# Decode attention on one Trainium2 core: one head per transfer, keys on partitions, whole-row softmax

## The chip, the cores and the metric

One core of a Trainium2 chip runs the whole program. The metric is device time in microseconds (us) of one execution. A core has TensorE (PE, with its weight loads shown apart as PEld), VectorE (DVE), ScalarE (ACT), GpSimd (POOL) and SyncE (SP), and 16 DMA engines that fill its on-chip memory.

## The reference

A layer norm of `x`, then attention with a K/V cache (one query per batch) and a SwiGLU network side by side, both added to `x`. Batch 4, width 512, 32 heads, 8192 keys of 128 numbers, all bf16:

```python
def _A_ref(x, k_cache, v_cache, wq, wo):          # B, Sq, D = 4, 1, 512;  H, Sk, Dh = 32, 8192, 128
    q = (lambda x, *d: x.transpose(*d))((x @ wq).reshape(B, Sq, H, Dh), 0, 2, 1, 3)
    scores = jnp.einsum("bhqd,bhkd->bhqk", q, k_cache) * (Dh ** -0.5)
    p = _softmax(scores, axis=-1)
    o = jnp.einsum("bhqk,bhkd->bhqd", p, v_cache)
    return (lambda x, *d: x.transpose(*d))(o, 0, 2, 1, 3).reshape(B, Sq, H * Dh) @ wo
def _B_ref(x, w_gate, w_up, w_down):              # F = 1792
    g = _silu(x @ w_gate)
    u = x @ w_up
    return (g * u) @ w_down
...
xn = _layernorm(x, axis=-1)
return x + _A_ref(xn, A_k_cache, A_v_cache, A_wq, A_wo) + _B_ref(xn, B_w_gate, B_w_up, B_w_down)
```

There are 4 x 32 = 128 pairs of a batch and a head, called heads here. Each has 2 MiB of K and 2 MiB of V, so 512 MiB of cache pass through the core once.

## The kernel before

It goes over the 8192 keys in four chunks `j` of 2048 (`CH`), and over all 128 heads within each chunk.

- `k_phase(j)` loads K for two heads (`HG`) of one batch with one 1 MiB transfer on SP's queue (tile `knat`, in runs of 4 KB). K comes with keys on partitions. TensorE turns each block of 128 keys by a transpose, K block stationary and an identity moving (line 231), into PSUM tiles `tps` of eight blocks. `evac` copies them to `kt`, three of five on DVE (line 113), two on ACT (line 115). Then the scores: q of the head, alone in a 32-column block `qpad`, is stationary, and 512 columns of `kt` move. Four batches use four column strips of the array, and the results add up in four PSUM tiles `sps`, with heads on partitions. All heads' scores of a chunk go to `s_buf`, with their running maximum.
- `softmax_phase(j)` is an online softmax for all 128 heads at once: new maximum, a factor `ccol` that rescales the output so far (`OT`) and the row sums (`RST`), exp on ACT (line 270), and transposes of the result (line 275), so that `pt_buf` has keys on partitions.
- `pv_phase(j)` loads V as K is loaded (tile `vt`) and multiplies: a 128x128 block of V is stationary, one column of `pt_buf` moves, and the result adds to a column of `OT` in PSUM tile `mp`.

All matmuls but the transposes go through one helper, `mm_acc` (line 118), and so have its line. After the first `k_phase`, the `pv_phase` of chunk j and the `k_phase` of chunk j+1 alternate, two heads of each batch at a time (a group `g`); the last `pv_phase` has no K beside it. There, `wo` is loaded on ACT's queue, and `finalize_group` normalizes and multiplies by it. The weights of the network are loaded at the start on ACT's queue and used before the first chunk. The order within each engine is that of the program; K and V tiles wait on SP for one of 5 (`knat`) or 8 (`vt`) buffers.

Of the kernel before, what the change touches and what calls it, by code (L numbers as in the profile page):

```python
# [8 lines left out]
dt = mybir.dt  # L10
# [6 lines left out]
def kernel(  # L17
# [20 lines left out]
    assert D % P == 0 and F % P == 0  # L38
# [3 lines left out]
    T = 16  # L42
    CH = P * T
    assert Sk % CH == 0
    NJ = Sk // CH
    HG = 2
    assert H % HG == 0
    NG = H // HG
    SB = 512
    NA = CH // SB  # L50
    assert NA * SB == CH and 32 * B == P
    EB = 1024
    assert CH % EB == 0 and EB % P == 0
    NEB = CH // EB
    TPB = EB // P
    assert T % TPB == 0
    NTC = CH // P
    eps = 1e-5
    qscale = float(Dh) ** -0.5
    NKN = 5  # L60
    NKT = 6
    NV = 8
    assert FC % 7 == 0
# [6 lines left out]
    v_pool = ctx.enter_context(tc.tile_pool(name="vnat", bufs=NV))  # L70
    psM = ctx.enter_context(tc.tile_pool(name="psM", bufs=1, space=bass.MemoryType.PSUM))
# [5 lines left out]
    ones_pb = const.tile([P, 1], dt.bfloat16, name="ones_pb")  # L77
    nc.vector.memset(ones_pb[:], 1.0)
    ones_row = const.tile([1, P], dt.float32, name="ones_row")
    nc.vector.memset(ones_row[:], 1.0)  # L80

    qpad = persist.tile([P, M * 32], dt.bfloat16, name="qpad")
    s_buf = [persist.tile([P, CH], dt.bfloat16, name=f"s_buf{i}") for i in range(2)]
    pt_buf = [persist.tile([P, NTC, P], dt.bfloat16, name=f"pt_buf{i}") for i in range(2)]
    xnt = persist.tile([P, EC, B], dt.bfloat16, name="xnt")
    yfx = persist.tile([B, D], dt.float32, name="yfx")
    cmaxj = persist.tile([P, 1], dt.float32, name="cmaxj")
    cmax4 = persist.tile([P, NA], dt.float32, name="cmax4")
    mrun = persist.tile([P, 1], dt.float32, name="mrun")
    mnew = persist.tile([P, 1], dt.float32, name="mnew")  # L90
    ccol = persist.tile([P, 1], dt.float32, name="ccol")
    nbias = persist.tile([P, 1], dt.float32, name="nbias")
    row_sb = persist.tile([1, P], dt.float32, name="row_sb")
    bc_sb = persist.tile([P, M], dt.float32, name="bc_sb")
    otn_sb = persist.tile([P, M], dt.bfloat16, name="otn_sb")

    mp = psM.tile([P, 512], dt.float32, name="mp")
    OT = mp[:, 0:M]
    BC = mp[:, 128:128 + M]
    RST = mp[0:1, 256:256 + M]  # L100
    CT = mp[0:1, 384:384 + M]
    nc.vector.memset(mp[:, 0:256], 0.0)
    nc.vector.memset(mp[0:1, 256:512], 0.0)

    nc.gpsimd.memset(qpad[:], 0.0)

    copy_i = [0]

    def evac(out_ap, in_ap):
        k = copy_i[0] % 5  # L110
        copy_i[0] += 1
        if k in (0, 2, 4):
            nc.vector.tensor_copy(out=out_ap, in_=in_ap)  # L113
        else:
            nc.scalar.copy(out=out_ap, in_=in_ap)  # L115

    def mm_acc(out_ap, lhsT, rhs, **kw):
        nc.tensor.matmul(out_ap, lhsT=lhsT, rhs=rhs, start=False, stop=False,  # L118
                         skip_group_check=True, **kw)

    def col_stride_ap(ap2d, start, count, step):
        return ap2d[:, start : start + step * (count - 1) + 1 : step]

    def bcast_row(row_src_ap):
        nc.vector.memset(BC, 0.0)
        mm_acc(BC, lhsT=ones_row[0:1, :], rhs=row_src_ap)
        nc.vector.tensor_copy(out=bc_sb[:], in_=BC)

    with tc.tile_pool(name="knat", bufs=NKN) as knat_pool, \
            tc.tile_pool(name="kt", bufs=NKT) as kt_pool, \  # L130
            tc.tile_pool(name="psT", bufs=3, space=bass.MemoryType.PSUM) as psT:
        with tc.tile_pool(name="p0sb", bufs=1) as p0, tc.tile_pool(name="p0ps", bufs=1, space=bass.MemoryType.PSUM) as p0ps:
            x_sb = p0.tile([B, D], dt.bfloat16, name="x_sb")
            nc.sync.dma_start(out=x_sb[:], in_=x_flat[:, :])
            wq_c, wg_c, wu_c = [], [], []
            for c in range(EC):
                t_ = kt_pool.tile([P, H * Dh], dt.bfloat16, name="kt")
                nc.sync.dma_start(out=t_[:], in_=A_wq[c * P:(c + 1) * P, :])
                wq_c.append(t_)
            for c in range(EC):  # L140
                t_ = knat_pool.tile([P, F], dt.bfloat16, name="knat")
                nc.scalar.dma_start(out=t_[:], in_=B_w_gate[c * P:(c + 1) * P, :])
                wg_c.append(t_)
            for c in range(EC):
                t_ = v_pool.tile([P, F], dt.bfloat16, name="vt")
                nc.scalar.dma_start(out=t_[:], in_=B_w_up[c * P:(c + 1) * P, :])
                wu_c.append(t_)
            wd_c = []
            for fc2 in range(0, FC, 7):
                t_ = v_pool.tile([P, 7, D], dt.bfloat16, name="vt")  # L150
                nc.scalar.dma_start(out=t_[:], in_=B_w_down[fc2 * P:(fc2 + 7) * P, :].rearrange(
                    "(fc p) e -> p fc e", p=P))
                wd_c.append(t_)

            xf = p0.tile([B, D], dt.float32, name="xf")
            nc.vector.tensor_copy(out=xf[:], in_=x_sb[:])
            xsum = p0.tile([B, 1], dt.float32, name="xsum")
            nc.vector.reduce_sum(out=xsum[:], in_=xf[:], axis=AX.X)
            mean = p0.tile([B, 1], dt.float32, name="mean")
            nc.vector.tensor_scalar(out=mean[:], in0=xsum[:], scalar1=1.0 / D, scalar2=None, op0=ALU.mult)  # L160
            xc = p0.tile([B, D], dt.float32, name="xc")
            nc.vector.tensor_scalar(out=xc[:], in0=xf[:], scalar1=mean[:, 0:1], scalar2=None, op0=ALU.subtract)
            sq = p0.tile([B, D], dt.float32, name="sq")
            nc.vector.tensor_tensor(out=sq[:], in0=xc[:], in1=xc[:], op=ALU.mult)
            vsum = p0.tile([B, 1], dt.float32, name="vsum")
            nc.vector.reduce_sum(out=vsum[:], in_=sq[:], axis=AX.X)
            epst = p0.tile([B, 1], dt.float32, name="epst")
            nc.vector.memset(epst[:], eps)
            std = p0.tile([B, 1], dt.float32, name="std")
            nc.scalar.activation(out=std[:], in_=vsum[:], func=ACT.Sqrt, bias=epst[:, 0:1], scale=1.0 / D)  # L170
            rstd = p0.tile([B, 1], dt.float32, name="rstd")
            nc.vector.reciprocal(out=rstd[:], in_=std[:])
            xn_bf = p0.tile([B, D], dt.bfloat16, name="xn_bf")
            nc.vector.tensor_scalar(out=xn_bf[:], in0=xc[:], scalar1=rstd[:, 0:1], scalar2=None, op0=ALU.mult)

            xnt_ps = p0ps.tile([P, EC, B], dt.bfloat16, name="xnt_ps")
            for c in range(EC):
                nc.tensor.transpose(xnt_ps[:, c, :], xn_bf[0:B, c * P:(c + 1) * P], ident[0:B, 0:B])
            nc.vector.tensor_copy(out=xnt[:], in_=xnt_ps[:])

            qt_ps = p0ps.tile([P, H * B], dt.float32, name="qt_ps")
            nc.vector.memset(qt_ps[:], 0.0)
            for h in range(H):
                for c in range(EC):
                    mm_acc(qt_ps[:, h * B:(h + 1) * B], lhsT=wq_c[c][:, h * Dh:(h + 1) * Dh], rhs=xnt[:, c, :])
            for b in range(B):
                dst = col_stride_ap(qpad[:], b * H * 32, H, 33)
                src = col_stride_ap(qt_ps[:], b, H, B)
                nc.vector.tensor_scalar(out=dst, in0=src, scalar1=qscale, scalar2=None, op0=ALU.mult)

            gu_ps = p0ps.tile([P, 2, FC * B], dt.float32, name="gu_ps")
            nc.vector.memset(gu_ps[:], 0.0)
            for fc in range(FC):
                for c in range(EC):
                    mm_acc(gu_ps[:, 0, fc * B:(fc + 1) * B], lhsT=wg_c[c][:, fc * P:(fc + 1) * P], rhs=xnt[:, c, :])
            for fc in range(FC):
                for c in range(EC):
                    mm_acc(gu_ps[:, 1, fc * B:(fc + 1) * B], lhsT=wu_c[c][:, fc * P:(fc + 1) * P], rhs=xnt[:, c, :])
# [8 lines left out]
            for fc in range(FC):  # L207
                mm_acc(yf_ps[0:B, :], lhsT=ht[:, fc * B:(fc + 1) * B], rhs=wd_c[fc // 7][:, fc % 7, :])
# [88 lines left out]
        def run_all(gen):  # L297
            for _ in gen:
                pass
# [66 lines left out]
```

## Time and profile before

| | |
|---|---|
| Runs | 1423.69 us median of 3 (1423.33 to 1423.88) |
| Profiled execution | span 1421.1 us from its first to its last instruction; its time outside the span is not in the profile, and the runs' median is 2.6 us longer |
| TensorE matmuls, busy | 1181.8 us (83%) |
| TensorE weight loads, busy | 896.6 us (63%) |
| DVE, ACT busy | 464.5 us (33%), 428.4 us (30%) |
| Moved by DMA | 553.37 MB, mean 389 GB/s |
| Mean granted TensorE clock | 0.829 |

In a profile row, `x` and a number is a count; "busy" is the union of the instructions' times, and "mean" that of one, in ns. A matmul's row names its stationary block as partitions*columns, then its output and its type. "PEclk" is the share of its full clock that TensorE was granted. A matmul's own duration includes its latency; in a burst, matmuls overlap, so the time each adds is less than its duration. After `[` stands the idle time ahead, and what ended it.

### The profile page before, as it was taken

The page shows a single profiled execution, that of the slowest core. Times are in us where ns is not written, and L with a number is a line of the kernel's source. Part 1 is how long each engine was busy: PE and PEld are TensorE (multiplying, and loading weights), DVE is VectorE, ACT ScalarE, POOL GpSimd, SP SyncE. Part 2 cuts the span into 40 slices and gives each one's busy share as a digit, 9 for nine tenths or more (in the row PEclk, how much of TensorE's full clock was granted, in tenths as well). Part 3 has the DMA queues.
Part 4 walks back from the last instruction along what each step waited for, and adds up shares of the span by engine and source line. Part 5 has one row for each costly group of instructions (what it writes and reads, how often), then busy time and mean ns, then how long its engine had stood idle before and what let it go on. Part 6 is the DMA issues. An engine that isn't in the chain of part 4 may idle for free.

```text
span 1421.1 us, 40337 instructions
## 1 busy us (share of the span) xinstructions
PE 1181.8 (83%) x18861; PEld 896.6 (63%) x18861; DVE 464.5 (33%) x790; ACT 428.4 (30%) x435; POOL 4.5 (0%) x9
## 2 busy tenths in 40 slices
PE   2999999899988988898898898799888889854454
PEld 2666666677766666676666666677666666643333
DVE  2444444433323332532233233433233323320000
ACT  0444445333323332432233233333223323310000
POOL 1000000000000000000000000000000000000000
PEclk9999999898888888898888788889888878855555
DMA  9988889899999999999999999999999999999997
GB/s 379 364 322 316 318 324 353 355 408 408 408 409 408 408 408 408 403 409 408 408 408 408 402 408 402 408 380 408 408 408 408 408 406 408 381 373 408 409 408 297
DMA packets 147158, 553.37 MB, mean 389 GB/s; under 512 B 8488, under 2 KB 14384, under 8 KB 146480
## 3 DMA queue, kind: packets, MB, share of 16 engines
q1 hardware_dynamic: 139856, 541.11, 96.3%
q10 hardware_dynamic: 7136, 9.70, 2.0%
q8 instruction: 147, 2.41, 0.7%
q14 instruction: 19, 0.16, 0.0%
HBM read 550.77 MB, written 0.00 MB: 388 GB/s over the span
## 4 chain that ended last, share of the span: by engine, by line
DMA 59%; PE 32%; ACT 3%; SPq 3%; DVE 1%; issue 1%; ACTq 0%
DMA knat<-in_A_k_cache_dram 47%; PE tps L231 18%; DMA vt<-in_A_v_cache_dram 10%; PE sps L118 9%; SPq L287 3%; ACT kt L115 3%; PE mp L118 3%; DMA wo_sb<-in_A_wo_dram 1%; DMA knat<-in_B_w_gate_dram 1%; DVE cmax L245 1%; PE pps L275 0%; DVE s_buf L113 0%; PE yf_ps L118 0%; PE qt_ps L118 0%; PE gu_ps L118 0%
## 5 line engine op out<-in xcount | busy, mean ns | idle before, releaser
L231 PE MATMUL tps<-ident,knat 128*128 128x128 bf16 x8192 | 603.8, 236 | 99.9 <-DMA knat<-in_A_k_cache_dram 78.5
L231 PEld LDWEIGHTS <-knat 128*128 128x128 bf16 x8192 | 537.7, 107 | 216.1 <-issue 127.0
L113 DVE COPY kt<-tps 128x1024 bf16<-128x1024 bf16 x615 | 412.9, 689 | 739.5 <-PE tps L231 500.8
L115 ACT COPY kt<-tps 128x1024 bf16<-128x1024 bf16 x409 | 407.5, 1013 | 770.8 <-PE tps L231 645.5
L118 PE MATMUL sps<-kt,qpad 128*32 128x512 bf16 x2048 | 336.3, 393 | 0.0
L118 PE MATMUL mp<-pt_buf,vt 128*128 128x1 bf16 x8192 | 233.1, 164 | 102.1 <-DMA vt<-in_A_v_cache_dram 93.8
L118 PEld LDWEIGHTS <-vt 128*128 128x128 bf16 x8248 | 222.7, 99 | 144.4 <-DMA vt<-in_A_v_cache_dram 114.0
L118 PEld LDWEIGHTS <-qpad 128*32 128x32 bf16 x2048 | 115.2, 97 | 117.6 <-issue 21.0
L325 DVE TENSOR_TENSOR otn_sb<-mp,bc_sb 128x2 bf16<-128x2 f32 x64 | 5.7, 152 | 151.2 <-PE mp L118 151.2
L118 PE MATMUL yo_ps<-wo_sb,otn_sb 128*4 128x512 bf16 x32 | 16.3, 612 | 7.2 <-DVE otn_sb L325 7.2
L275 PE MATMUL pps<-ident,s_buf 128*128 128x128 bf16 x64 | 8.2, 310 | 7.6 <-ACT s_buf L270 7.6
L260 PE MATMUL mp<-ident_f,ccol 128*1 128x128 f32 x3 | 1.1, 373 | 13.6 <-ACT ccol L257 13.6
L275 PEld LDWEIGHTS <-s_buf 128*128 128x128 bf16 x64 | 6.2, 140 | 9.5 <-ACT s_buf L270 9.3
L245 DVE TENSOR_REDUCE cmax<-s_buf 128x1 f32<-128x512 bf16 x16 | 10.1, 674 | 0.2
L260 PEld LDWEIGHTS mp<-ident_f,ccol 128*1 128x1 f32 x3 | 0.2, 79 | 15.1 <-ACT ccol L257 15.1
L270 ACT ACTIVATE s_buf<-s_buf,nbias 128x1024 bf16<-128x1024 bf16 x8 | 8.7, 1140 | 3.0 <-issue 2.0
L216 DVE MEMSET sps<- 128x512 f32 x16 | 7.8, 485 | 2.5 <-ACT pt_buf L115 1.4
L118 PE MATMUL mp<-pt_buf,ones_pb 128*1 128x128 bf16 x64 | 6.9, 284 | 0.2 <-ACT pt_buf L115 0.2
L113 DVE CAST s_buf<-sps 128x512 bf16<-128x512 f32 x9 | 6.1, 686 | 3.0 <-PE sps L118 3.0
L118 PEld LDWEIGHTS <-otn_sb 128*4 128x4 bf16 x32 | 1.5, 87 | 8.6 <-DVE otn_sb L325 8.6
L170 ACT ACT_TABLE_LOAD x1 | 1.3, 1283 | 18.5 <-DMA vt<-in_B_w_up_dram 18.5
L118 PEld LDWEIGHTS <-ones_pb 128*1 128x1 bf16 x64 | 5.6, 111 | 1.4 <-issue 1.3
(64 smaller groups left out, 62.4 us busy)
## 6 DMA issues: line engine op xcount, KB each, us to landing
knat<-in_A_k_cache_dram SPq DMA_DIRECT2D x256, 1024.0 KB, 17.9
vt<-in_A_v_cache_dram SPq DMA_DIRECT2D x256, 1024.0 KB, 18.6
kt<-in_A_wq_dram SPq DMA_DIRECT2D x4, 1024.0 KB, 9.0
wo_sb<-in_A_wo_dram ACTq DMA_DIRECT2D x4, 1024.0 KB, 18.6
knat<-in_B_w_gate_dram ACTq DMA_DIRECT2D x4, 448.0 KB, 11.0
vt<-in_B_w_up_dram ACTq DMA_DIRECT2D x4, 448.0 KB, 13.7
vt<-in_B_w_down_dram ACTq DMA_DIRECT2D x2, 896.0 KB, 21.4
x_sb<-in_A_x_dram SPq DMA_DIRECT2D x1, 4.0 KB
```

The lines of the kernel that those rows point to most:

```text
L113: nc.vector.tensor_copy(out=out_ap, in_=in_ap)
L115: nc.scalar.copy(out=out_ap, in_=in_ap)
L118: nc.tensor.matmul(out_ap, lhsT=lhsT, rhs=rhs, start=False, stop=False, skip_group_check=True, **kw)
L170: nc.scalar.activation(out=std[:], in_=vsum[:], func=ACT.Sqrt, bias=epst[:, 0:1], scale=1.0 / D)
L216: nc.vector.memset(s_t[:], 0.0)
L231: nc.tensor.transpose(tps[:, u, :], knat[:, h, t, :], ident[:, :])
L245: nc.vector.tensor_reduce(out=cmax4[:, a:a + 1], in_=s_sb[:, a * SB:(a + 1) * SB], axis=AX.X, op=ALU.max)
L260: nc.tensor.matmul(CT, lhsT=ccol[:, 0:1], rhs=ident_f[:, :], is_transpose=True, start=False, stop=False, skip_group_check=True)
L270: nc.scalar.activation(out=s_sb[:, cs], in_=s_sb[:, cs], func=ACT.Exp, bias=nbias[:, 0:1], scale=1.0)
L275: nc.tensor.transpose(pps[:, u, :], s_sb[:, nt * P:(nt + 1) * P], ident[:, :])
L287: nc.sync.dma_start(out=vt[:], in_=src)
L325: nc.vector.tensor_tensor(out=otn_sb[:, m0:m0 + HG], in0=OT[:, m0:m0 + HG], in1=bc_sb[:, m0:m0 + HG], op=ALU.mult)
```

## The change

The loop over chunks goes. The kernel now walks over the 128 heads once, `i` from 0, in a fixed order per engine written out in the program.

- **Transfers.** `load_k` and `load_v` fetch a whole head with one 2 MiB transfer on SP; each partition gets 64 keys in a run of 16 KB. K, V and the weights share one pool of nine 16 KB-per-partition buffers (`slots`). K is loaded two heads ahead; V of head `i` is issued at step `i` and used at step `i + 2` (`LAGV`). The last V comes in four parts.
- **Scores.** Per head, eight groups `g` of eight blocks: transposes as before (`t_group`), copies to `kt` (five on DVE, three on ACT), and two groups later (`LAGS`) `s_group`: the transposed K block, 128x128, is stationary, and the single column of q moves. So the scores have keys on partitions, a 128 x 64 tile per head.
- **Softmax.** One pass per head over the whole row: `max_1` (DVE), `max_2` (an f32 transpose of one column on TensorE, then a DVE maximum), `max_3` (an f32 matmul that spreads the negative scaled maximum to all partitions, a DVE copy, exp on ACT with the row sums). No transposes of the result and no rescaling. `row_sums`, `fin_1` and `fin_2` follow once per four heads.
- **PV.** `pv_group`: V stationary and one column moving, as before.
- **Order.** In each group: transposes of head `i`, scores two groups behind, PV of head `i - 2`, then the softmax steps of head `i - 1`.
- **Network and output weights.** The network's weights come on SP at step 1, and `do_ffn` runs ahead of step 4, its sigmoid made of an exp and a reciprocal. `wo` comes in four parts at steps 3 to 6.

The core of the new text:

```python
GT = 8; NGR = T // GT; NSLOT = 9; LAGV = 2; LAGS = 2          # T = Sk // P = 64
slots  = ctx.enter_context(tc.tile_pool(name="slots", bufs=NSLOT))
kt_pool = ctx.enter_context(tc.tile_pool(name="ktp", bufs=9))
psT = ctx.enter_context(tc.tile_pool(name="psT", bufs=3, space=bass.MemoryType.PSUM))
psS = ctx.enter_context(tc.tile_pool(name="psS", bufs=2, space=bass.MemoryType.PSUM))
ctx.enter_context(tc.manual_schedule())
...
def load_k(m):
    h, b = divmod(m, B)
    t_ = slot()
    nc.sync.dma_start(out=t_[:], in_=A_k_cache[b, h, :, :].rearrange("(p t) d -> p (t d)", p=P))
    k_tiles[m] = t_[:].rearrange("p (t d) -> p t d", d=Dh)
...
on_dve = (True, False, True, True, False, True, False, True)
def t_group(m, g):
    tps = psT.tile([P, GT, P], dt.bfloat16, name="tps")
    for u in range(GT):
        nc.tensor.transpose(tps[:, u, :], k_tiles[m][:, g * GT + u, :], ident[:, :])
    kt = kt_pool.tile([P, GT, P], dt.bfloat16, name="kt")
    if on_dve[g]:
        nc.vector.tensor_copy(out=kt[:], in_=tps[:])
    else:
        nc.scalar.copy(out=kt[:], in_=tps[:])
    kts[m, g] = kt

def s_group(m, g):
    if g == 0:
        s_ps[m] = psS.tile([P, 512], dt.float32, name="sps")
    kt = kts.pop((m, g))
    for u in range(GT):
        t = g * GT + u
        mm(s_ps[m][:, t:t + 1], kt[:, u, :], qt[:, m:m + 1], start=True)

def max_1(m):
    mx = small.tile([P, 1], dt.float32, name="mx")
    nc.vector.reduce_max(out=mx[:], in_=s_ps[m][:, 0:T], axis=AX.X)
    sc[m] = mx
def max_2(m):
    nc.tensor.matmul(s_ps[m][0:1, C_MX:C_MX + P], lhsT=sc[m][:, 0:1], rhs=ident_f[:, :], is_transpose=True,
                     start=True, stop=True, skip_group_check=True)
    gm = small.tile([1, 1], dt.float32, name="gm")
    nc.vector.reduce_max(out=gm[:], in_=s_ps[m][0:1, C_MX:C_MX + P], axis=AX.X)
    sc[m] = gm
def max_3(m):
    mm(s_ps[m][:, C_NB:C_NB + 1], nscale_row[0:1, :], sc.pop(m)[0:1, 0:1], start=True)
    nb = small.tile([P, 1], dt.float32, name="nb")
    nc.vector.tensor_copy(out=nb[:], in_=s_ps[m][:, C_NB:C_NB + 1])
    p_ = small.tile([P, T], dt.bfloat16, name="p_sb")
    nc.scalar.activation(out=p_[:], in_=s_ps[m][:, 0:T], func=ACT.Exp, bias=nb[:, 0:1], scale=qscale,
                         accum_out=rs[:, m:m + 1])
    p_sb[m] = p_
...
def pv_group(m, g):
    ...
        mm(o_ps[h][:, b:b + 1], v_tiles[m][:, t, :], p_sb[m][:, t:t + 1], start=(b == 0 and t == 0))
...
for i in range(M + LAGV + 1):
    if i + 2 < M:
        load_k(i + 2)
    if i < M:
        load_v(i, parts=4 if i == M - 1 else 1)
    if i == 1:
        load_ffn()
    if i == 4:
        do_ffn()
    if 3 <= i < 7:
        load_wo(i - 3, 4)
    for g in range(NGR):
        if i < M:
            t_group(i, g)
        ms = i if g >= LAGS else i - 1
        if 0 <= ms < M:
            s_group(ms, (g - LAGS) % NGR)
        mp = i - LAGV
        if 0 <= mp < M:
            pv_group(mp, g)
        mx = i - 1
        if 0 <= mx < M:
            if g == LAGS:
                max_1(mx)
            if g == LAGS + 1:
                max_2(mx)
            if g == LAGS + 3:
                max_3(mx)
            if g == LAGS + 5 and mx % B == B - 1:
                row_sums(mx)
        mf = i - LAGV - 1
        if 0 <= mf < M and mf % B == B - 1:
            if g == 0:
                fin_1(mf // B)
            if g == 1:
                fin_2(mf // B)
```

More of the change, by code (lines that the diff above doesn't have):

```diff
@@ L76 @@
     make_identity(nc, ident_f[:])
[L77 to L84, printed above, removed]
-    xnt = persist.tile([P, EC, B], dt.bfloat16, name="xnt")
@@ L95 @@
[L95 to L192, printed above, removed]
@@ new lines @@
+    for c in range(EC):
+        nc.tensor.transpose(xnt_ps[:, c, :], xn_bf[0:B, c:D:EC], ident[0:B, 0:B])
+    xnt = persist.tile([P, EC, B], dt.bfloat16, name="xnt")
+    nc.vector.tensor_copy(out=xnt[:], in_=xnt_ps[:])
+    qt_ps = psT.tile([P, M], dt.float32, name="tps")
+    for h in range(H):
+        for c in range(EC):
+            lhsT = wq_t[c // 2][:, (c % 2) * H * Dh + h * Dh:(c % 2) * H * Dh + (h + 1) * Dh]
+            mm(qt_ps[:, h * B:(h + 1) * B], lhsT, xnt[:, c, :], start=(h == 0 and c == 0))
@@ L193, with do_ffn @@
+    def do_ffn():
+        wg, wu, wd = ffn["w"]
+        gu_ps = psT.tile([P, 2, FC * B], dt.float32, name="tps")
+        for i, w in enumerate((wg, wu)):
             for fc in range(FC):
                 for c in range(EC):
[L195 to L198, printed above, removed]
@@ new lines, in do_ffn @@
+        gs = persist.tile([P, FC * B], dt.float32, name="gs")
+        nc.vector.tensor_tensor(out=gs[:], in0=gu_ps[:, 0, :], in1=sig[:], op=ALU.mult)
+        ht = persist.tile([P, FC * B], dt.bfloat16, name="ht")
+        nc.vector.tensor_tensor(out=ht[:], in0=gs[:], in1=gu_ps[:, 1, :], op=ALU.mult)
+        yf_ps = psT.tile([B, D], dt.float32, name="tps")
+        for fc in range(FC):
+            mm(yf_ps[0:B, :], ht[:, fc * B:(fc + 1) * B], wd[:, fc, :], start=(fc == 0))
+        nc.vector.tensor_tensor(out=yfx[:], in0=yf_ps[0:B, :], in1=xf[:], op=ALU.add)
@@ new lines, in fin_2 @@
+    def fin_2(h):
+        mm(yo_ps[0:B, :], sc.pop(("otn", h))[:, :], wo_sb[:, h, :], start=(h == 0))
+    for i in range(M + LAGV + 1):
[34 more added lines that the diff above has]
+                    fin_2(mf // B)
```

267 lines of the change are left out of this document (108 added, 159 removed).

## The prediction

> **What bounds the kernel now.** I read the page's engine totals and slices first, then busy time by stage, then single bursts, and last the clock. Rows of the page:
>
> ```profile
> PE 1181.8 (83%) x18861; PEld 896.6 (63%) x18861; DVE 464.5 (33%) x790; ACT 428.4 (30%) x435; POOL 4.5 (0%) x9
> PEclk9999999898888888898888788889888878855555
> GB/s 379 364 322 316 318 324 353 355 408 408 408 409 408 408 408 408 403 409 408 408 408 408 402 408 402 408 380 408 408 408 408 408 406 408 381 373 408 409 408 297
> DMA packets 147158, 553.37 MB, mean 389 GB/s; under 512 B 8488, under 2 KB 14384, under 8 KB 146480
> HBM read 550.77 MB, written 0.00 MB: 388 GB/s over the span
> L231 PE MATMUL tps<-ident,knat 128*128 128x128 bf16 x8192 | 603.8, 236 | 99.9 <-DMA knat<-in_A_k_cache_dram 78.5
> L113 DVE COPY kt<-tps 128x1024 bf16<-128x1024 bf16 x615 | 412.9, 689 | 739.5 <-PE tps L231 500.8
> L115 ACT COPY kt<-tps 128x1024 bf16<-128x1024 bf16 x409 | 407.5, 1013 | 770.8 <-PE tps L231 645.5
> L118 PE MATMUL sps<-kt,qpad 128*32 128x512 bf16 x2048 | 336.3, 393 | 0.0
> L118 PE MATMUL mp<-pt_buf,vt 128*128 128x1 bf16 x8192 | 233.1, 164 | 102.1 <-DMA vt<-in_A_v_cache_dram 93.8
> ```
>
> The bytes are fixed by the reference, and nearly all packets are under 8 KB (K and V move in 4 KB runs). The rows of the three costly matmuls and two copies are the bricks used below. The stages (time, busy of PE, weight loads, DVE, ACT, POOL, granted clock, DMA share, GB/s):
>
> ```profile
> 44.00:250.00 206.00, 199.52 (x2495) 141.16 (x2494) 101.90 (x154) 98.93 (x101) 0.00 (x0) 1.00 0.88 330
> 262.00:1236.00 974.00, 864.35 (x13773) 666.61 (x13770) 324.39 (x503) 308.76 (x313) 0.00 (x0) 0.84 1.02 404
> 1236.00:1411.00 175.00, 91.70 (x2148) 68.76 (x2146) 18.78 (x89) 9.08 (x10) 0.00 (x0) 0.54 1.01 395
> ```
>
> The first stage (K only) is bound by TensorE, 97% busy with the DMA at 330 GB/s. The rest is bound by the DMA at 404 and 395, and TensorE's clock is only partly granted there. At the 408 GB/s of the page's slices, 550.77 MB need 1350 us; the span is 1421.1, the median of the runs 1423.69, so 2.6 us lie outside the span.
>
> **The bricks.** Per head of K and V (4 MiB, 10.3 us of DMA at 408) the changed kernel still makes 64 transposes (8192 / 128) and 64 matmuls with V stationary. Its scores turn from 16 matmuls of 512 columns into 64 with a 128x128 stationary block and one moving column: the form of today's V matmuls. So two bricks carry the sum, at both clocks:
>
> ```profile
> 49.64 1.51 PE L231 MATMUL tps<-ident,knat 128*128 128x128 bf16 x24
> 1084.27 3.60 PE tps L231 x32
> 975.35 3.35 PE L118 MATMUL mp<-pt_buf,vt 128*128 128x1 bf16 x128
> 1300.25 1.01 PE L118 MATMUL mp<-pt_buf,vt 128*128 128x1 bf16 x32 [1.56 <-DMA vt<-in_A_v_cache_dram]
> ```
>
> Less one latency (0.24 and 0.16 us, the page's means), a transpose takes (1.51-0.24)/23 = 55 ns at full clock and (3.60-0.24)/31 = 108 at half. A one-column matmul with its load takes (3.35-0.16)/127 = 25 ns at full, (1.01-0.16)/31 = 27 at half. A head's 64 transposes and 128 one-column matmuls are 6.7 us at full clock, but 64 x 0.108 + 128 x 0.027 = 10.4 us at half: as much as its DMA. Everything hangs on which clock this mix is granted.
>
> **The clock.** It changes in steps 3.41 us apart. I cut windows at these steps; each pair is a window and its successor, all instructions:
>
> ```profile
> 958.17:961.58 3.41, 3.41 (x127) 3.41 (x124) 0.00 (x0) 0.06 (x1) 0.00 (x0) 1.00 1.02 408
> 961.58:964.99 3.41, 3.41 (x26) 2.34 (x23) 1.38 (x2) 1.97 (x2) 0.00 (x0) 0.50 1.03 407
> 333.53:336.94 3.41, 3.41 (x65) 3.41 (x62) 0.52 (x1) 1.01 (x1) 0.00 (x0) 0.50 1.02 405
> 336.94:340.36 3.42, 3.42 (x21) 1.83 (x19) 0.87 (x2) 1.01 (x1) 0.00 (x0) 0.50 1.03 411
> 374.49:377.90 3.41, 2.77 (x27) 2.77 (x28) 0.69 (x1) 1.01 (x1) 0.00 (x0) 0.50 1.03 410
> 377.90:381.32 3.42, 3.42 (x45) 2.49 (x44) 1.85 (x3) 1.89 (x2) 0.00 (x0) 1.00 1.02 407
> ```
>
> And the transposes alone in three of them and in a fourth (time, PE, loads, clock, DMA):
>
> ```profile
> 958.17:961.58 3.41, 0.74 (x14) 0.77 (x15) 1.00 1.02 408
> 333.53:336.94 3.41, 2.48 (x24) 2.50 (x25) 0.50 1.02 405
> 374.49:377.90 3.41, 2.77 (x27) 2.77 (x28) 0.50 1.03 410
> 1207.34:1210.76 3.42, 2.43 (x24) 2.44 (x25) 0.50 1.02 402
> ```
>
> At 958 TensorE is busy the whole window, 14 transposes and 113 one-column matmuls, and still loses its clock. At 333 it is busy the whole window at half clock, 24 transposes and 41 one-column matmuls, and is not woken; at 374, 27 transposes with pauses wake it. So what counts is columns streamed: one-column matmuls and weight loads count next to nothing, and waking takes 25 to 27 transposes a window.
>
> Now the new mix. At half clock a dense head of 11.6 us (below) gives 64 x 3.41 / 11.6 = 19 transposes a window: under the 24 that failed, so a clock once lost does not return. At full clock a head would take about 8 us, be done before its DMA (9.9 to 10.3) and pause some 2 us in one piece, waiting for V: a window with that pause holds (3.41-2)/8 x 64 = 11 transposes, fewer than the 14 that lost the clock. I expect half clock from about head 8 on.
>
> The Trainium skill (TensorE: Matmul & The Clock Gate, Part 4) says that transposes do not count as busy for the clock gate in the same way. By that rule the clock would be low as well; the trace disagrees with it, since 27 transposes alone wake the clock.
>
> **The sum, part by part.**
> - Scores: 2048 wide matmuls (336.3 us) go, 8192 x 27 ns = 221 us come; in the 10.4.
> - Whole-row softmax, per head: one f32 transpose, one f32 matmul with a 128-column f32 stationary, per four heads a row sum and one 512-column output matmul. Rows:
>
> ```profile
> 581.22 0.37 PE L260 MATMUL mp<-ident_f,ccol 128*1 128x128 f32 x1 [4.22 <-ACT ccol L257]
> 582.22 0.50 PEld L118 LDWEIGHTS mp<-row_sb,ones_row 1*128 1x128 f32 x2 [0.93 <-DVE mp L125]
> L118 PE MATMUL yo_ps<-wo_sb,otn_sb 128*4 128x512 bf16 x32 | 16.3, 612 | 7.2 <-DVE otn_sb L325 7.2
> 51.08 1.90 PE L118 MATMUL sps<-kt,qpad 128*32 128x512 bf16 x20
> 52.92 1.51 PE L231 MATMUL tps<-ident,knat 128*128 128x128 bf16 x24
> L245 DVE TENSOR_REDUCE cmax<-s_buf 128x1 f32<-128x512 bf16 x16 | 10.1, 674 | 0.2
> L270 ACT ACTIVATE s_buf<-s_buf,nbias 128x1024 bf16<-128x1024 bf16 x8 | 8.7, 1140 | 3.0 <-issue 2.0
> 37.52 4.38 PE L118 MATMUL yf_ps<-vt,ht 128*4 128x512 bf16 x14 [0.30 <-DVE ht L204]
> ```
>
>   The f32 transpose is 0.37 less a latency of 0.16, 0.2 us; the two f32 loads 0.4 (0.50 less their overlap); the four-head work an output matmul of 0.4 (0.61 less the same latency, as half clock has it), a row sum like the f32 matmul, 0.4, and 0.2 of changes, over 4: 0.25. A change of the stationary block's shape costs about 0.1: the last of the 20 score matmuls at 51.08 starts 0.39 (its mean) before their end at 52.98, streams 0.21, and the transposes start at 52.92, 0.12 later. In and out of the f32 transpose and of the f32 matmul that is four times 0.1. Together 0.2 + 0.4 + 0.25 + 0.4 = 1.25 us, so a head is 10.4 + 1.25 = 11.6. Bounds: 0.5 (the loads and the transpose overlapped, no changes) and 2.3 (eight changes from transposes to scores at 0.13 besides), so 10.9 to 12.7. I take 11.6, because scores and V matmuls share the full 128x128 shape with the transposes, and no row shows a cost between those.
> - New waits: scores wait for a copy two groups back, some 2.6 us at half clock against 0.69 or 1.01 of copy; the max chain's steps lie one or two groups (1.3 us each) apart, against one copy (0.69) and one reduce of 64 or 128 columns, under the 0.67 that 512 columns take (L245). Behind a late one would stand the next group's transposes. Taken as 0; If that cover is gone, each step left open costs TensorE up to 0.7 a head, 83 us over 119 heads, inside the upper bound. Neither engine is near its limit: DVE copies 5 x 0.69 = 3.5 us a head and at most 3 x 0.67 more, ACT 3 x 1.01 = 3.0 and an exp under the 1.14 of 1024 columns (L270), of 11.6.
> - Transfers: twice the size, 16 KB runs instead of 4 KB. While wq arrived in 8 KB runs the rate was higher:
>
> ```profile
> 8.00:10.00 2.00, 0.00 (x0) 0.00 (x0) 0.18 (x1) 0.00 (x0) 0.00 (x0) 1.00 1.00 417
> 10.00:12.00 2.00, 0.00 (x0) 0.00 (x0) 0.00 (x0) 0.00 (x0) 0.00 (x0) 1.00 1.04 433
> ```
>
>   I take 424, 408 as the other bound: 9.9 to 10.3 us a head, under 11.6, so worth nothing behind a slow TensorE. With nine slots SP issues K and V some three heads ahead, then waits for PV to free slots.
> - FFN weights (5.5 MB, 13 us of queue) move from ACT's queue to SP, behind V1 and ahead of K4; its matmuls move ahead of head 4: 112 four-column ones of 27 ns (3 us), a sigmoid chain I put at 1.5, and 14 of 512 columns (the 4.38 row, part of it at half clock), together 9 us of TensorE with which nothing else there overlaps. wo (4.2 MB, 10 us of queue) moves from the start of the last V stage into heads 3 to 6. Both delay K and V while TensorE is behind anyway.
> - Gone: the 330 GB/s stage, the softmax breaks and the V-only stage, in all 71 us above the 1350.
>
> Timeline: wq and K0 (6.3 MB at 424, and 2 us to the first byte) land near 17 us. Heads 0 to 3 run at half clock: head 0 has no V yet (64 x 0.108 + 64 x 0.027 = 8.6), head 1 has the extras too (9.9), then 11.6 twice. They end near 59, FFN 68, whose 512-column matmuls wake the clock; heads 4 and 5 at 8 us, 84; then V is late, and TensorE waits for it: V6 is there after 46.4 MB at 112 (wq, nine K, seven V, FFN, three quarters of wo), and head 8, which needs it, ends at 124. If the clock is lost two heads earlier or later, this point hardly moves. From there 119 heads x 11.6 = 1380, end 8 (last scores, max chain, 128 one-column matmuls, output, an estimate), outside 2.6: **1515 us**. With 10.9 and 12.7 it is 1432 and 1646.
>
> **Rivals.**
> 1. Other side: the clock stays full, and the DMA binds throughout. Then 550.77 MB at 424 are 1299, plus 2 at the start, 6 at the end, 2.6: 1310; at 408, 1361. It decides if pauses of 2 us and 21 transposes a window on average keep the clock. For it: the K stage at 1.00 with few pauses. Against: the window at 958, lost without any pause. The Trainium skill (TensorE: Matmul & The Clock Gate, "Why this matters for your kernels") has the rule that only pauses above about 3 us drop the clock; by it this rival wins, and the window at 958 speaks against it.
> 2. The clock alternates, as in the middle stage now (0.84), because the f32 and 512-column matmuls tip some windows: a head of (11.6 + 9.9)/2 = 10.75 gives 1414. Against: even with four transposes' worth added, 19 stays under 24.
> 3. Half clock, but the softmax extras hide wholly: 10.4 a head, 1372. Against: the f32 loads go through the same TensorE.
> 4. Shape changes cost more than my bound, or a max-chain wait stands open: over 1646.
>
> **Chances.** Forecast (1432 to 1646) 0.70; rival 1 0.15 (0.10 at 1310, 0.05 at 1361); rival 2 0.08; rival 3 0.03; rival 4 0.04. The range of all is 1355 to 1640, which leaves out the 424 case and the top; the likeliest case's own is 1432 to 1646. A measurement here tells about 0.2% from no change: faster 0.24 (rivals 1, 3 and most of 2), same 0.02, slower 0.74.
>
> **What would show it.** Right: PEclk 5 in nearly all slices after the first few, TensorE busy near 100%, transposes at a mean near 310 ns, GB/s falling to about 360, SP waiting for slots. Wrong: PEclk mostly 9, or idle of TensorE ended by DMA throughout with GB/s at 408 or more. Score matmuls spaced well over 27 ns, or idle ahead of max_2 or max_3, would show the extras mis-sized.

## The result, and the profile after

The changed kernel takes 1378.27 us (median of 4 runs, 1377.07 to 1378.53) against 1423.54 for the kernel before on the same chip: ratio 0.968, 95% interval 0.967 to 0.969. It is faster by 3.2%, where 1515 us, slower than before, had been forecast. Where runs of one version differ by more than 1.5%, the time given below is that of its fast runs alone; the two versions without V have one such run each, and their profiles are of longer runs. The profiled execution's span is 1376.8 us. The page of the kernel after, with the rows that answer to those of before:

```profile
PE 1304.3 (95%) x25314; PEld 1271.9 (92%) x25314; DVE 517.0 (38%) x1107; ACT 443.6 (32%) x644; POOL 1.1 (0%) x8
PEclk9675855785765765585767765556757558556666
GB/s 395 427 404 420 424 424 427 425 424 426 423 425 426 409 425 396 396 426 404 402 426 409 424 424 406 380 374 381 417 425 421 409 387 413 421 374 403 416 400 65
DMA packets 42412, 554.21 MB, mean 403 GB/s; under 512 B 4296, under 2 KB 8400, under 8 KB 8912
q8 instruction: 197, 3.23, 0.9%
PE 88%; DMA 9%; issue 3%; SPq 0%; DVE 0%; ACT 0%; ACTq 0%
L201 PE MATMUL tps<-ident,slot 128*128 128x128 bf16 x8192 | 907.1, 279 | 15.7 <-issue 12.0
L66 PE MATMUL sps<-qt,kt 128*128 128x1 bf16 x8192 | 389.8, 168 | 8.4 <-issue 7.5
L66 PE MATMUL ops<-p_sb,slot 128*128 128x1 bf16 x8192 | 355.8, 164 | 30.0 <-issue 16.6
L66 PE MATMUL sps<-gm,nscale_row 1*128 1x1 f32 x256 | 63.2, 314 | 0.0
L226 PE MATMUL sps<-ident_f,mx 128*1 128x128 f32 x128 | 43.6, 341 | 0.2 <-DVE mx L222 0.2
```

TensorE is the bound: 88% of the chain that ended last, 95% busy. The 4 KB packets are gone (42412 packets, 147158 before), and the transfers run at 424 to 427 GB/s wherever the queue is full. But the clock row isn't 5 throughout: after the first slices it goes up and down between 5 and 8. The transposes' mean is 279 ns, between 236 (before) and the 310 that half clock throughout was to give. The waits that involve TensorE, in us in total, times, longest (the largest such rows):

```profile
PEld L66 <- issue: 31.3, 39, 1.9
PEld L201 <- issue: 24.3, 46, 1.9
PE ops L66 <- issue: 16.6, 15, 1.8
PE ops L66 <- DMA slot<-in_A_v_cache_dram: 13.3, 9, 4.0
PE tps L201 <- issue: 12.0, 13, 1.7
```

TensorE hardly waits for V (9 times). More often it waits for nothing that the profile shows ("issue"). These pauses are short, and they turn out to matter more than their sum. Transposes alone, in windows cut at the 3.41 us steps of the clock (columns: busy time and count of PE and of weight loads, granted clock, DMA share, GB/s; a transpose that an edge of the window cuts is counted in both windows):

```profile
238.37:241.78 3.41, 2.88 (x24) 2.12 (x22) 0.50 1.01 423
241.78:245.20 3.42, 2.08 (x16) 1.67 (x16) 0.50 1.04 441
838.98:842.39 3.41, 2.39 (x19) 1.71 (x17) 0.50 0.96 408
842.39:845.81 3.42, 2.37 (x20) 1.89 (x21) 0.50 0.99 417
845.81:849.22 3.41, 2.29 (x21) 1.78 (x19) 0.50 1.01 404
849.22:852.63 3.41, 2.53 (x21) 1.85 (x18) 0.50 0.97 411
252.02:255.43 3.41, 2.71 (x24) 2.21 (x22) 0.50 1.02 428
255.43:258.85 3.42, 1.99 (x26) 1.44 (x24) 1.00 1.00 426
265.68:269.09 3.41, 1.48 (x19) 1.00 (x20) 1.00 1.03 432
269.09:272.50 3.41, 2.71 (x24) 2.21 (x22) 0.50 0.99 418
272.50:275.92 3.42, 2.08 (x28) 1.48 (x27) 1.00 1.02 431
```

Four half-clock windows with 19 to 21 transposes wake nothing. Two with 24 (at 252 and 269, each with an f32 transpose of the maximum besides) are each followed by a window at full clock; one with 24 and no f32 transpose (at 238) is not. Counted up to 1360 us, 18 of the 25 half-clock windows that show 23 or 24 transposes and an f32 one are followed by full clock, and 7 of the 35 that show 24 without one. Of those with 23 and no f32 transpose none is, and of those with fewer one alone, that with the network's 512-column matmuls. So 23 to 24 is the edge, and at the edge the count alone doesn't decide. The same edge holds at full clock: of the windows with 24 or more transposes 80 of 84 keep the clock, of those with fewer 1 of 23. The window at 265.68 runs at full clock, has only 19, and loses the clock. TensorE's timeline inside it:

```profile
264.80 0.61 PE L201 MATMUL tps<-ident,slot 128*128 128x128 bf16 x8
265.65 0.61 PE L201 MATMUL tps<-ident,slot 128*128 128x128 bf16 x8
266.50 0.55 PE L201 MATMUL tps<-ident,slot 128*128 128x128 bf16 x7
268.12 0.22 PE L201 MATMUL tps<-ident,slot 128*128 128x128 bf16 x1 [1.07 <-issue]
268.95 0.94 PE L201 MATMUL tps<-ident,slot 128*128 128x128 bf16 x8
270.17 1.01 PE L201 MATMUL tps<-ident,slot 128*128 128x128 bf16 x8
```

Groups start 0.85 us apart at full clock and 1.22 at half. The one pause of 1.07 us ("issue", after the seventh transpose of a group) takes more than a group's transposes out of its window, and the next window is at half clock.

In all, the clock is full for 382 us and half for 973. Each fall between 269 and 1338 us comes with an issue pause of 0.8 to 1.9 us that begins in the window before it (21 falls); of the first five, four come with a wait for K or V. Not every pause costs the clock: one of 1.19 us that ends at 750.74, across the edge of two windows, does not. The 59 heads that lie wholly at half clock take 11.4 us each (11.05, or 11.48 with the row sums, or 11.66 with the output matmul); full-clock heads without a wait take 7.3 to 7.9. From head 9 (127.2 us) to head 127 (1360.5) a head takes 10.45 on average.

### The profile page after: what moved, and what is told of

It reads as the page before. It is cut to its first block, busy times and chain, and to the rows that moved or that the text cites. A ratio compares the mean times of both kernels' runs of the same rounds, so it can differ in the third digit from the quotient of the medians.

```text
span 1376.8 us, 53655 instructions
## 1 busy us (share of the span) xinstructions
PE 1304.3 (95%) x25314; PEld 1271.9 (92%) x25314; DVE 517.0 (38%) x1107; ACT 443.6 (32%) x644; POOL 1.1 (0%) x8
## 2 busy tenths in 40 slices
DMA packets 42412, 554.21 MB, mean 403 GB/s; under 512 B 4296, under 2 KB 8400, under 8 KB 8912
## 4 chain that ended last, share of the span: by engine, by line
PE 88%; DMA 9%; issue 3%; SPq 0%; DVE 0%; ACT 0%; ACTq 0%
PE tps L201 53%; PE sps L66 17%; PE ops L66 15%; DMA slot<-in_A_v_cache_dram 7%; DMA slot<-in_A_k_cache_dram 2%; PE sps L226 2%; PE yo_ps L66 1%; SPq L87 0%; SPq L79 0%; DVE res L305 0%; SPq L74 0%; ACT p_sb L237 0%; DVE otn L260 0%; DVE nb L235 0%; ACTq L332 0%
## 5 line engine op out<-in xcount | busy, mean ns | idle before, releaser
L201 PE MATMUL tps<-ident,slot 128*128 128x128 bf16 x8192 | 907.1, 279 | 15.7 <-issue 12.0
L201 PEld LDWEIGHTS <-slot 128*128 128x128 bf16 x8192 | 699.4, 126 | 35.1 <-issue 24.3
L66 PEld LDWEIGHTS <-kt 128*128 128x128 bf16 x8192 | 388.8, 109 | 10.7 <-issue 9.7
L66 PE MATMUL sps<-qt,kt 128*128 128x1 bf16 x8192 | 389.8, 168 | 8.4 <-issue 7.5
L66 PE MATMUL ops<-p_sb,slot 128*128 128x1 bf16 x8192 | 355.8, 164 | 30.0 <-issue 16.6
L66 PEld LDWEIGHTS <-slot 128*128 128x128 bf16 x8432 | 301.2, 102 | 39.0 <-issue 18.0
L237 ACT ACTIVATE p_sb<-sps,nb 128x64 bf16<-128x64 f32 x128 | 40.2, 314 | 151.5 <-DVE nb L235 151.5
L66 PE MATMUL sps<-gm,nscale_row 1*128 1x1 f32 x256 | 63.2, 314 | 0.0
L66 PEld LDWEIGHTS sps<-gm,nscale_row 1*128 1x128 f32 x256 | 52.3, 253 | 3.1 <-DVE kt L204 1.0
L226 PE MATMUL sps<-ident_f,mx 128*1 128x128 f32 x128 | 43.6, 341 | 0.2 <-DVE mx L222 0.2
L229 DVE TENSOR_REDUCE gm<-sps 1x1 f32<-1x128 f32 x128 | 35.3, 276 | 5.0 <-PE sps L226 5.0
L66 PE MATMUL tps<-xnt,slot 128*128 128x4 bf16 x240 | 10.6, 182 | 6.4 <-DMA slot<-in_A_wq_dram 6.4
```

The costliest lines, as they stand in the source:

```text
L66: nc.tensor.matmul(out_ap, lhsT=lhsT, rhs=rhs, start=start, stop=True, skip_group_check=True, **kw)
L201: nc.tensor.transpose(tps[:, u, :], k_tiles[m][:, g * GT + u, :], ident[:, :])
L226: nc.tensor.matmul(s_ps[m][0:1, C_MX:C_MX + P], lhsT=sc[m][:, 0:1], rhs=ident_f[:, :], is_transpose=True, start=True, stop=True, skip_grou ...
L229: nc.vector.reduce_max(out=gm[:], in_=s_ps[m][0:1, C_MX:C_MX + P], axis=AX.X)
L237: nc.scalar.activation(out=p_[:], in_=s_ps[m][:, 0:T], func=ACT.Exp, bias=nb[:, 0:1], scale=qscale, accum_out=rs[:, m:m + 1])
```

## The experiments

Letters stand for theories as the expectations use them; C is the clock theory (the columns that TensorE streams in one 3.41 us window decide its clock). They also call fill 4 `e1_fill4`, wide 8 `e5_wide8`, the order of four order-4, and the changed kernel without V e14. Fillers write a tile that is overwritten at once. Each ratio is against the kernel before.

**Fill 4.** Half of each group's transposes are made twice.

```diff
-        for u in range(GT):
+        for u in (*range(4), *range(GT)):
             nc.tensor.transpose(tps[:, u, :], k_tiles[m][:, g * GT + u, :], ident[:, :])
```

> Four of the eight transposes of each group are made twice (same data, same place): 32 more per head, nothing else changed. Theory C (the granted clock follows streamed columns, and the clock is what costs): at full clock a head takes about 9.4 us, under the 9.9 of its DMA, TensorE has hardly a pause, 33 transposes a window, so PEclk above 0.9, DMA-bound at 424 GB/s: 1305 to 1335 us, although TensorE has half as many transposes again. Rival W (TensorE's work binds at whatever clock the change brings): 32 x 0.055 to 0.108 more per head at the same mean clock 0.65, 1378 + 128 x 2.6 = about 1700; anything over 1500 supports W.

Measured 1440.84, ratio 1.014 (1.011 to 1.016). The clock rose to 0.93 as C says, and the time rose as well: it lies in neither range. The page:

```profile
PEclk9899999988999899999998899999999899999988
PE 87%; issue 9%; DMA 4%; DVE 0%; SPq 0%; ACT 0%; ACTq 0%; DVEq 0%
q8 instruction: 230, 3.77, 1.0%
```

Issue is 9% of the chain, and the queue q8 carries the instructions: 230 packets of 16 KB. TensorE's 58820 loads and matmuls (29410 of each) over 230 are 256, so a packet is 128 load-matmul pairs. Their starts in the trace lie 6.25 us apart at full clock (median). That 230 x 6.25 is 1437, near the span of 1439.3, proves nothing by itself, since the packets are spread over the span whatever binds. The place of the pauses tells more: all 95 issue pauses of over 0.6 us after 100 us begin after a multiple of 128 pairs and the same 94 more, and end 1.2 to 1.7 us after a packet has landed. So do all 29 such pauses in the changed kernel. So a full-clock TensorE out-ran its instructions.

**Wide 8.** The same 512 columns a group, as one matmul in place of four transposes.

```diff
         tps = psT.tile([P, GT, P], dt.bfloat16, name="tps")
+        mm(tps[:].rearrange("p a b -> p (a b)").bitcast(dt.float32), ident[:, :],
+           k_tiles[m][:, g * GT:g * GT + 4, :], start=True)
```

> Ahead of each group's transposes one matmul of 512 columns (identity stationary, K moving) whose result is overwritten: the same 512 streamed columns a group as the four repeated transposes of e1_fill4, but one weight load and matmul instead of four. Theory I (at full clock TensorE is short of instructions: a 16 KB fetch, 128 load-matmul pairs, lands every 6.25 us, and e1_fill4's 228 pairs a head need 11.1 us): 204 pairs a head need at most 10.0, about the DMA's 9.9, so PEclk above 0.9, DMA-bound, 1310 to 1345 us. Rival W (the streamed work itself binds e1_fill4): same columns, same time, 1425 to 1450 us.

Measured 1340.94, ratio 0.942 (0.941 to 0.944), 100 us less than fill 4 for the same columns: theory I. The page:

```profile
PEclk9888999999999999999999998999999999999998
q8 instruction: 206, 3.38, 1.0%
DMA 58%; PE 40%; issue 1%; SPq 0%; DVE 0%; ACT 0%; ACTq 0%; DVEq 0%
```

TensorE does more, its clock is granted (0.97), and the DMA becomes the bound.

**Scores twice.** Each one-column score matmul is made twice.

```diff
-        for u in range(GT):
+        for u in (*range(GT),) * 2:
             t = g * GT + u
             mm(s_ps[m][:, t:t + 1], kt[:, u, :], qt[:, m:m + 1], start=True)
```

> Each one-column score matmul is made twice (same value, same place): 64 more per head, about 1.7 us of TensorE at either clock, but hardly a streamed column. Theory C: fewer transposes per window (64 x 3.41 / 13.0 = 17 at half clock), so hardly any waking: PEclk 0.50 to 0.55, 13.0 us a head, 1580 to 1680 us. Rival B (the clock follows busy time of TensorE, of whatever kind): TensorE is busier and pauses less, PEclk above 0.65, under 1450 us.

Measured 1699.82, ratio 1.194 (1.192 to 1.196), clock 0.514, half-clock heads of 12.8 to 13.4. The clock came as C says; the time is 20 us above its range. One-column matmuls take time and don't wake: with 64 x 27 ns more a head, windows hold fewer transposes (none shows 24), and the clock stays down. This is what had been predicted for the change itself, some 1.7 us a head away from it.

```profile
PEclk9655555555555555555555555555555555555555
```

**Order of four.** The same instructions; four groups of transposes in a row, then four of scores, then four of PV.

```diff
-        for g in range(NGR):
-            if i < M:
-                t_group(i, g)
+        for g0 in (0, 4):
+            for g in range(g0, g0 + 4):
+                if i < M:
+                    t_group(i, g)
...
+                for g in range(g0, g0 + 4):
+                    s_group(ms, (g - 4) % NGR)
...
+                for g in range(g0, g0 + 4):
+                    pv_group(mp, g)
```

> Same instructions, other order: four groups of transposes in a row, then four groups of scores (four groups behind instead of two), then four of PV. Theory C: four groups in a row stream 32 x 0.107 = 3.4 us of columns at half clock, so most heads hold a window above the 25 or so that wake the clock; PEclk 0.75 to 0.9, 1310 to 1350 us. Rival: order does not matter since the mean over a head is the same: PEclk 0.65, 1370 to 1390 us.

Measured 1337.96, ratio 0.940 (0.938 to 0.941), clock 0.745. Nothing but the order changed; 32 transposes in a row at 108 ns fill a window (3.5 us). The clock is lost more often than in the changed kernel and comes back much sooner: 95 stretches at half clock with a median of 6.8 us, the longest 20.5, against 27 with a median of 20.5, the longest 140. Most of these falls (53 of 95) have no pause of over 0.5 us beside them: a window that is filled with scores and PV has few transposes. So it is the count that loses the clock, not the pause as such. The DMA is the bound:

```profile
PEclk9676777687777777877768678767877767787766
DMA 72%; PE 26%; ACT 1%; issue 1%; SPq 0%; DVE 0%; DVEq 0%
```

This is the fastest of the versions that compute everything; two with fillers lie within 3 us.

**No maximum.** The row maximum is replaced by a constant 0, so its f32 transpose, f32 matmul and two reduces are gone.

```diff
-        mm(s_ps[m][:, C_NB:C_NB + 1], nscale_row[0:1, :], sc.pop(m)[0:1, 0:1], start=True)
-        nb = small.tile([P, 1], dt.float32, name="nb")
-        nc.vector.tensor_copy(out=nb[:], in_=s_ps[m][:, C_NB:C_NB + 1])
+        nb = nb0
...
-                if g == LAGS:
-                    max_1(mx)
-                if g == LAGS + 1:
-                    max_2(mx)
```

> The row maximum is left out (exp with bias 0; the softmax is the same in exact arithmetic): max_1, max_2 and max_3 go, so no f32 transpose and no f32 matmul per head, 0.66 us of TensorE at half clock. Theory C, with the f32 transpose as the drop that tips windows of three transposing groups over the threshold: without it the fullest windows hold 24 transposes, so the clock seldom wakes: PEclk 0.50 to 0.56, 10.5 us a head, 1365 to 1395 us. Rival (waking has another cause than these columns): PEclk 0.65 or more and the time falls by half to all of 128 x 0.66, to 1290 to 1340 us.

Measured 1345.13 (1339 to 1351), ratio 0.945 (0.942 to 0.948), clock 0.60, half-clock heads 10.6: between the two. The clock wakes without the f32 transpose: 21 of the 93 half-clock windows that show 24 bf16 ones do it, and of those with fewer only one, with the network's matmuls. In the changed kernel 18 of the 25 wakings that lack the network's matmuls came with one: it helps, and isn't needed.

**Fillers and orders combined.** Wide 8 without the maximum, then three in one set: order of four without the maximum; order of four with a 512-column filler ahead of each run of transposes; fillers in every second group without the maximum.

> e5_wide8 without the row maximum (exp with bias 0): three pairs and 0.4 us of TensorE less per head at full clock. If e5_wide8 is bound by the DMA, the time is within 10 us of it; if TensorE or its instructions still bind there, 15 to 60 us less.

> The order of four groups, with the row maximum left out (a constant 0 stands in its place, so one f32 transpose, one f32 matmul and two reduces a head are gone). By the clock theory (C) windows of order-4 hold runs of 32 transposes in a row and wake without the f32 transpose: granted clock 0.7 to 0.9, and the time is that of the DMA, 550.77 MB at 424 GB/s = 1299 us plus about 12 at the ends: 1310 to 1340. If the f32 transpose of the maximum was what woke the clock, it stays near 0.5 and the time is the half-clock head's without extras, 10.6 us x 119: over 1380.

> The order of four groups with the maximum kept, and one filler matmul of 512 columns ahead of each run of transposes (two a head, their output is overwritten). Clock theory: fewer windows fall, granted clock 0.85 to 0.97 against 0.745 without the fillers; since the DMA is on the chain for 72% there already, the time gains little: 1320 to 1340. If the clock were still what sets the time in that order, the gain would be over 15 us (under 1322).

> The changed kernel's own order, with one 512-column filler in every second group (four a head) and the row maximum left out. Clock theory: half the filler columns are enough to wake the clock again after each pause, because a window then holds 16 to 24 transposes and one or two fillers: granted clock 0.8 to 0.95, time 1320 to 1345, as with eight fillers. If the clock needs a filler in each group, the clock is 0.6 to 0.7 and the time stays near 1345, that without maximum and fillers.

Measured 1337.30 (clock 0.96), 1335.24 (0.76), 1339.40 (0.82) and 1337.98 (0.84); ratios 0.940, 0.938, 0.941, 0.940, each interval within 0.002. All four times came as expected; the clock of the third is below its 0.85. With clocks from 0.76 to 0.96 they lie within 5 us: past the point where the DMA binds, more clock buys nothing.

**Runs of 4 KB.** The changed kernel, and wide 8, with K and V in 4 KB runs inside the same 2 MiB transfers.

```diff
-        nc.sync.dma_start(out=t_[:], in_=A_k_cache[b, h, :, :].rearrange("(p t) d -> p (t d)", p=P))
+        nc.sync.dma_start(out=t_[:].rearrange("p (j w) -> p j w", j=4),
+                          in_=A_k_cache[b, h, :, :].rearrange("(j p t) d -> p j (t d)", j=4, p=P))
```

> e5_wide8 with K and V in four runs of 4 KB per partition in the same 2 MiB transfer, instead of one of 16 KB. Theory D (longer runs carry the rate from 408 to 424 GB/s): 550.77 MB need 1350 us, so 1355 to 1375, some 45 above e5_wide8 if that is DMA-bound. Rival: run length does not matter: within 10 us of e5_wide8.

> The changed kernel with runs of 4 KB, nothing else. Theory: its mean head of 10.45 us lies just above the 10.3 that the DMA then needs, so full-clock stretches run into the DMA: 1385 to 1410 us. If the time stays within 5 us of 1378, the longer runs gave this kernel nothing.

Measured 1392.85 for wide 8 (52 us more than with 16 KB runs) and 1397.84 for the changed kernel (20 more). The second is in its range; the first is 18 us above it: at the 403 GB/s of its median slice the bytes need 1367 us, not 1350. Slices of the first:

```profile
GB/s 381 414 397 399 407 407 406 407 407 407 403 405 406 402 404 397 402 407 403 402 404 394 401 406 403 403 406 394 403 407 403 398 408 398 401 407 405 402 400 242
DMA 85%; PE 13%; SPq 1%; DVE 0%; issue 0%; ACT 0%; ACTq 0%; DVEq 0%
```

So the length of the runs, not the size of the transfer, carries the rate from at most 408 to 424. It is worth 50 us where the DMA binds and 20 in the changed kernel, where TensorE binds most of the time.

**Wide 8, scores twice.** 268 pairs a head at a granted clock.

> Eight 512-column fillers a head and every score matmul made twice, so 268 pairs of weight load and matmul a head. Instruction theory (I): at full clock TensorE gets 128 pairs per 6.25 us, 48.8 ns a pair, so 13.1 us a head and 1650 to 1730 us in all, with the chain at 'issue' and a granted clock over 0.8. Without such a limit, full-clock work is 64 x 0.055 + 192 x 0.025 + 8 x 0.21 + 0.9 = 10.9 us a head: 1400 to 1450 us. At half clock the work is 64 x 0.108 + 192 x 0.027 + 8 x 0.43 + 1.1 = 16.6 us a head: over 1950 us.

Measured 1682.44 (1661.8 to 1682.8), ratio 1.177 (1.169 to 1.185). The number is that of theory I (269 packets x 6.25 = 1681), but in part by luck, since the time is made up otherwise in the trace: issue is 4% of its chain, not most of it. 56 of its heads lie at full clock (11.3 on average, many at 10.6 to 11.4), near TensorE's own work of 10.9; 71 lie partly (14.0 on average) or wholly (16.4) at half clock. The clock is lost at fetches here as well (35 of 37 falls come with an issue pause). That costs more than the 59 issue pauses of over 0.5 us themselves, 62 us in all: 64 heads partly at half clock take 2.7 us more each than the full-clock ones.

```profile
PEclk9686897798899798789778977979897778597979
GB/s 400 421 407 389 324 364 306 326 356 341 349 351 373 302 307 346 309 339 361 303 320 331 361 317 299 375 329 331 367 334 308 302 310 330 267 360 332 315 306 50
PE 94%; issue 4%; DMA 1%; DVE 0%; SPq 0%; ACT 0%; ACTq 0%; DVEq 0%
```

**Without V, and without K and V.** Is the fetch slow by itself, or because K and V fill the 16 DMA engines? V isn't loaded in the first two (PV reads the K tile); in the third, K comes for two heads only as well. Every instruction of TensorE stays.

```diff
     def load_v(m, parts=1):
-        h, b = divmod(m, B)
-        t_ = slot()
...
+        v_tiles[m] = k_tiles[m]
     def load_k(m):
+        if m >= 2:                        # the third alone
+            k_tiles[m] = k_tiles[m % 2]
+            return
```

> Eight fillers and doubled scores as before (268 pairs a head), but V isn't loaded: PV reads the K tile in its place, which halves the bytes and leaves every TensorE instruction. If the fetch pace of 6.25 us per 128 pairs is the chip's own (F), 269 fetches take 1681 us and the time stays at 1640 to 1700. If the fetch is slow because it waits behind the K and V transfers (Q), it gets quicker with the queue mostly empty, and the time goes to TensorE's own work, 10.9 us a head: 1400 to 1480.

> The changed kernel with V not loaded (PV reads the K tile), nothing else changed. By F the pauses at the fetches stay, the clock alternates as before (0.6 to 0.7), and the time is 1340 to 1380. By Q the pauses go, no window falls, the granted clock is over 0.9 and a head takes 8 us: 1030 to 1100.

> The changed kernel with K loaded for heads 0 and 1 only (the later heads read those two tiles) and V not at all (PV reads the K tile); all instructions of TensorE stay. If the transfers' traffic is the whole cause of the fetch pauses (Q), no pause of 'issue' is left in the middle, the clock isn't lost, a head takes the dense full-clock 7.3 to 7.7 us: 128 x 7.5 + 30 = 970 to 1010 us, granted clock over 0.95. If the pauses and the falls of the clock stay with an idle queue, the clock alternates as in e14 and the time is over 1150.

Measured 1467.8, 1234.1 and 997.93 (997.1 to 998.7). The first lies in the range of Q, near its top; the second lies between the theories, and neither loses its pauses. The trace of the first says why. At full clock, instruction packets start 3.6 us apart (median, some 150 intervals) where the K transfers take under 60% of the DMA engines, and 6.0 to 7.1 (83 intervals) where they take more. K alone still fills the engines half the time (50.9% of the span). In the second, 20 of 22 falls of the clock come with an issue pause. The last run settles it:

```profile
PEclk9869999999999999999999999999999999999998
DMA  9900000000000000000000000000000000000000
q8 instruction: 198, 3.24, 1.3%
PE 97%; DMA 2%; ACT 0%; issue 0%; DVE 0%; SPq 0%; ACTq 0%; DVEq 0%
```

The same instructions and as many packets (197 and 198); with the engines all but free of transfers there is no issue on the chain, TensorE has no issue pause of over 0.5 us after 100 us, the clock stays full from 65 to 990 us, and nearly all heads take 7.28 to 7.67 us. So in the changed kernel the pauses, and the falls of the clock that come with them, are those of instruction fetches that compete with the K and V transfers. Which part of a fetch gets slow isn't shown.

## Why the prediction was wrong

- **What held.** The bricks: half-clock heads take 11.4 us against 11.6, full-clock ones 7.3 to 7.9 against "about 8". The rate of 424. The bound: TensorE, 88% of the chain, waits for the max chain under 1 us in all. The start: head 9 begins at 127.2, against 124. The clock's rule: columns count, one-column matmuls don't (scores twice).
- **The step that failed** is "19 transposes a window: under the 24 that failed, so a clock once lost does not return". 19 was a mean over a dense head, of transposes begun in a window, and 24 a count that takes in those cut by its edges: in the changed kernel's half-clock windows the first is 19.4 and the second 21.1. And windows spread about the mean: most groups of eight come 1.2 to 1.3 us apart, which doesn't divide 3.41, so single windows show 15 to 24. Of those that show 23 or 24, 25 woke the clock, 18 of them with an f32 transpose. With 59 of 127 heads wholly at half clock instead of all, a head took 10.45 instead of 11.6; 119 x 1.15 is 137, the whole miss (1515 - 1378).
- **Its bound was too sharp.** The row at 333.53 of before (24, not woken) was read as a floor for any mix. It holds for most windows with 24 and no f32 transpose (28 of 35), not for all; in the kernel without the maximum 21 of 93 woke it.
- **Which way the clock is lost** was wrong too. That a full-clock head would "pause some 2 us in one piece, waiting for V" holds for the first falls alone; later waits for V are rare (9 in all). The pauses are at instruction fetches, which no step of the prediction had. The Trainium skill (TensorE: Matmul & The Clock Gate, "Why this matters for your kernels") asks for no TensorE gap above about 3 us; here gaps of 0.8 to 1.9 us are enough. The Trainium skill (TensorE: Matmul & The Clock Gate, Part 4) has transposes not counting as busy in the same way; order of four, which only puts transposes in a row, raises the clock from 0.65 to 0.745.
- **The rivals.** Rival 2 is what happened, dismissed at 0.08. Its 10.75 a head is near 10.45, and its ground (f32 and 512-column matmuls tip windows) holds for 19 of the 26 wakings; the others come without them. The case against it used the same mean. Rival 1 (1310) did not happen; versions whose DMA binds come near it (1335 to 1341).

So the gain of 45 us is the difference of two things: the transfers' longer runs and the missing stages would give some 85 (1338, when TensorE keeps up), and TensorE's clock gives back 40 of them.

## What to carry to other kernels

Where a rule works window by window, compare the windows' spread with the threshold, not the mean, and count both in the same way: a mean below it doesn't keep windows from crossing. Instructions that count for the clock do more in one run than spread out, at the same work: the order alone was worth 40 us here. When a fully unrolled kernel of tiny matmuls runs beside saturated transfers, count its instruction packets and their spacing; fewer, wider instructions can be faster than less work.

## What the runs showed of the hardware

- Instructions come to TensorE in 16 KB packets of 128 load-matmul pairs, over the same DMA engines as the data. With the engines full they start 6.25 us apart at full clock (49 ns a pair, twice the 25 ns that a one-column pair takes); with K's transfers on under 60% of the engines, 3.6. With hardly any transfers TensorE's own need of one per 4.9 us (7.44 x 128 / 196, by the mean head and its pairs) is met.
- The clock is decided window by window of 3.41 us. In the changed kernel 80 of 84 full-clock windows with 24 or more 128-column transposes kept it and 1 of 23 with fewer; at half clock 23 to 24 are the least that woke it. One-column matmuls hardly count (scores twice). A pause of 0.8 to 1.9 us was enough to lose it 21 times.
- In the same 2 MiB transfers, runs of 16 KB move at 424 GB/s in the median slice of the versions that the DMA binds, and runs of 4 KB at 403.
- Open: the 24 to 30 us between the DMA-bound versions (1335 to 1341) and the DMA's own 1299 + 12. Their last slice of 33 us moves 151 to 188 GB/s, so a large part of it lies there, where TensorE still has two heads to do behind the last V; a shorter lag wasn't tried.
